# Issuing one low half of x behind a step's first addition, and one pair's first weight words behind an addition too

## The chip, the cores and the metric

The kernel runs on one core of a Trainium2 chip. The metric is the device time in microseconds (us) of one execution; shown runs of one kernel are compared by their median.

## The reference, cut to what matters

A channel attention over 6016 tokens and 256 channels, then two feed-forward layers with 2048 hidden units each:

```
s = kn.T @ qn / tau ; a = softmax(s) ; x = v @ a          # 6016 x 256
x = g1(x @ w_in) @ w_out      ; g1(h) = h * sigmoid(1.702 h)
x = g2(x @ w2_in) @ w2_out    ; g2(h) = max(0.01 h, h)
```

All inputs and the output are float32. The kernel splits each operand of a product into a rounded high half and a low half (the rest) and adds three products: high with high, low with high, high with low.

## The kernel before, in words

**Tiling.** The tokens are cut into six pairs of two column blocks, 512 columns wide each, 448 in the last pair. The two layers make twelve passes, numbered `i` from 0 to 11 (`i` of 6 and more is layer two). This text calls a pass a pair: pair 5 is the last of layer one, pair 11 the last of layer two. Each pair runs eight steps, `f` from 0 to 7; a step makes 2 x 128 hidden rows out of 256 channels. The hidden rows are made with seven block products in place of eight (a Strassen scheme): the blocks of x are combined beforehand (B11, T1, T2, T3 in `xa`, B21, B22, T4 in `xb`). From pair 3 on the output side works in the same way (`strassen_step`, L1292); pairs 1 and 2 use a simpler form (`step`, L1176).

**Engines.** TensorE (PE) makes all products. ScalarE (ACT) copies out of PSUM, applies the activation and makes high halves. VectorE (DVE) adds, subtracts and makes low halves (`subtract`, all recorded on L106, or L103 inside `halves`). Each engine works through its own instructions in the order in which the program issues them; that order is written out by hand (`manual_schedule`).

**One step of layer two** (L1292 to L1386), as it is issued: product A11, copy, product S2, copy to `tv`, product A12, its activation, product S3, copy to `tt`, `run_casts`, then `between(i, f)` (work for the next pair), product S1, and then the step's first addition on DVE, `add(g[:, 2], tt, pa)` at L1321. Behind it come the activation, the high half `g0[0]`, `next_stage()` (here the third stage of the step before: one DVE subtraction of 128x1024), `beyond(i, f)`, which empties the list `after`, then two output products, product S4, and the second addition `add(g[:, 1], tv, pa)`. S4 writes the same PSUM bank `pa` that the first addition reads.

**Next pair's x in layer two** (L1575 to L1601, called for pairs 5 to 10). The four blocks of the next pair lie in the staging tile `stg`. In steps 1 to 6 `more(j, n)` adds a block from HBM into block j of `stg` by an accumulating DMA on GpSimd's queue (POOL, L1579). `cast` makes a high half on ACT (L1512). `low` makes a low half on DVE, and `low_by_dma` makes it with an ACT copy (L1521) and an accumulating DMA on POOL's queue (L1524). In step 4 the order is: `low` of T3 out of block 1, `more(1, 0)` into the same block 1, `cast` of T1 out of block 0, `low_by_dma` of T1. In step 5, `cast(x, i, T2, 1)` reads block 1 after that `more`.

**Weights of layer two** are prepared during pairs 1 and 2. `begin_next` (L467) calls `words_of` for one weight piece: two DVE instructions put the words together (`bits`, L248 and L255), the load of a later piece is issued on SP, and `casts` gets the ACT work for `run_casts`. It is called at the end of each step of pair 1 and of steps 0 to 6 of pair 2. Between pair 1 and pair 2 `switch` (L1006) makes three blocks of `xb`: three casts on ACT and three low halves on DVE (L103).

**On the output side** `rest.pop(0)()` in `between` may transpose one output block on DVE (L1487) and store it with four DMAs (L1490); for pairs 7 to 10 one of these falls into step 4, ahead of `low`.

Of the kernel before, what the change touches and what calls it, by code (L numbers as in the profile page):

```python
# [17 lines left out]
def tile_kernel(  # L18
# [33 lines left out]
    NF = F // P // 2  # L52
# [39 lines left out]
    def bank(tag):  # L92
        return ps.tile([P, BLK], F32, tag=tag, name=tag)
# [28 lines left out]
    B11, T2, T1, T3 = range(4)  # L122
# [3 lines left out]
    with tc.manual_schedule():  # L126
# [324 lines left out]
        def run_casts():  # L451
            todo = list(casts)
            casts.clear()
            for item in todo:
                item()
# [11 lines left out]
        def begin_next():  # L467
            if words_left:
                words_of(words_left.pop(0))
# [636 lines left out]
                used.add(g)  # L1106

        coming = [prefetch(1, 1)]
        turn, streams = [], []

        def fetch():
            next(coming[0], None)
# [31 lines left out]
        def kept(tag, w):  # L1144
            return early.tile([P, BLK], F32, tag=tag, name=tag)[:, :w]
# [20 lines left out]
        def next_stage():  # L1166
            if stages:
                stages.pop(0)()
# [7 lines left out]
        def step(i, f):  # L1176

            layer, p = steps[i]
            w = width[p]
            product = products(i, f)  # L1180
            pa, pb = (bank(f"h{i}")[:, :w] for i in range(2))
            tp, tv, tt = (kept(tag, w) for tag in ("tp", "tv", "tt"))
            product(pa, A11, B11)
            nc.scalar.copy(pb, pa)
            while turn:
                turn.pop(0)()
            next_stage()
            slots.extend(lambda item=item, kc=kc: put(item, kc) for item in pend for kc in range(KC))
            pend.clear()
            outputs(2)  # L1190
            product(pb, S2, T2, more=True)
            nc.scalar.copy(tv, pb)
            product(pa, A12, B21, more=True)
            act(layer, tp, pa)
            hook("copy")
            next_stage()
            outputs(1)
            product(pb, S3, T3, more=True)
            nc.scalar.copy(tt, pb)
            run_casts()  # L1200
            between(i, f)
            product(pa, S1, T1)
            hook("burst")
            add(tt, tt, pa)
            if beside:
                beside.pop(0)()
            g11 = late.tile([P, 2, BLK], F32R, tag="gs", name="g11", bufs=2)[:, :, :w]
            g22 = late.tile([P, 2, BLK], F32R, tag="gq", name="g22")[:, :, :w]
            nc.scalar.copy(g11[:, 0], tp)
            subtract(g11[:, 1], tp, g11[:, 0].bitcast(F32))  # L1210
            act(layer, tt, tt)
            nc.scalar.copy(g22[:, 0], tt)
            next_stage()
            hook("one")
            beyond(i, f)
            outputs(2)
            hook("two")
            cc = late.tile([P, 2, BLK], F32, tag="cc", name="cc")[:, :, :w]
            product(pa, S4, B22, more=True)
            add(cc[:, 0], tv, pa)  # L1220
            close()
            hook("join")
            product(pb, A22, T4, more=True)
            act(layer, cc[:, 1], pb)
            subtract(g22[:, 1], tt, g22[:, 0].bitcast(F32))
            act(layer, cc[:, 0], cc[:, 0])
            if layer == 1:
                run_due()
                fetch()
                while streams:  # L1230
                    streams.pop()()
            outputs(len(slots))
            pend.append((layer, p, 1, f + NF, g22[:, 0], g22[:, 1]))
            pend.append((layer, p, 0, f, g11[:, 0], g11[:, 1]))

            def finish_step():
                gd = late.tile([P, 2, 2, BLK], F32R, tag="gd", name="gd", bufs=2)[:, :, :, :w]
                halves(gd[:, 0], gd[:, 1], cc)
                pend.append((layer, p, 1, f, gd[:, 0, 0], gd[:, 1, 0]))
                pend.append((layer, p, 0, f + NF, gd[:, 0, 1], gd[:, 1, 1]))  # L1240

            stages.append(finish_step)
            if f < NF - 1 or i == 1:
                begin_next()
            fetch()

        sets = [0]
# [266 lines left out]
        def low(to, i, n, j):  # L1514
            w = width[i % NPAIR]
            subtract(to[:, 1, n, :w], staged_x[i][:, j], to[:, 0, n, :w].bitcast(F32))
# [12 lines left out]
        def between(i, f):  # L1529
            if i < FIRST:  # L1530
                return
            k = NF * i + f
            if k >= NF * FIRST + 1:
                stream_in(k + 2)
            if k >= NF * FIRST + 2:
                stream_out(k + 1)
            if f == 0:
                if i == FIRST and i + 1 < NPAIR:
                    for n in range(2):
                        load_v(i + 1, n)  # L1540
                if i > FIRST:
                    cast(xbt, i, B22, 3)
                    cast(xbt, i, T4, t4_of(i))
                return
            if rest:
                rest.pop(0)()
            if f == 3 and i in (FIRST, NPAIR):
                raw_weights(steps[i][0])
            if i == LAST:
                return  # L1550
            i += 1
            x = xa[i % 2]
            first = 3
            if i < NPAIR:
                if f == 1 and i > FIRST + 1:
                    for n in range(2):
                        load_v(i, n)
                if f == 2:
                    move_in(i)
                    place_v(i, 0)  # L1560

                    def second_of_v():
                        place_v(i, 1)
                        for n in range(2, 4):
                            load_v(i, n)

                    after.append(second_of_v)
                if f == 3:
                    after.append(lambda: place_v(i, 2))
                if f == 4:  # L1570
                    place_v(i, 3)
            elif f == 1 and i not in staged_x:
                move_in(i)
            t = staged_x.get(i)
            if i >= NPAIR:  # L1575
                p = i - NPAIR

                def more(j, n):
                    nc.gpsimd.dma_start(out=t[:, j], in_=x2[p][:, n], accum_op=ALU.add)  # L1579

                if f == 1:
                    more(1, 3)
                if f == 2:
                    cast(x, i, B11, 0)
                    low_by_dma(x, i, B11, 0, x2[p][:, 0])
                if f == 3:
                    more(0, 1)
                    cast(x, i, T3, 1)
                if f == 4:
                    low(x, i, T3, 1)  # L1590
                    more(1, 0)
                    cast(x, i, T1, 0)
                    low_by_dma(x, i, T1, 0)
                if f == 5:
                    cast(x, i, T2, 1)
                if f == 6:
                    low(x, i, T2, 1)
                    more(1, 2)
                if f == 7:
                    cast(xbt, i, B21, 2)  # L1600
                return  # L1601
            if f == first:
                cast(x, i, B11, 0)
                low_by_dma(x, i, B11, 0)
            if f == first + 1:

                def sums_of_x():
                    subtract(t[:, 0], t[:, 1], t[:, 0])
                    cast(x, i, T1, 0)

                after.append(sums_of_x)
            if f == first + 2:
                low_by_dma(x, i, T1, 0)

                def sums_of_x():
                    subtract(t[:, 1], t[:, 3], t[:, 1])
                    cast(x, i, T3, 1)

                after.append(sums_of_x)
            if f == first + 3:  # L1620
                low_by_dma(x, i, T3, 1)

                def sums_of_x():
                    subtract(t[:, 0], t[:, 3], t[:, 0])
                    cast(x, i, T2, 0)

                after.append(sums_of_x)
            if f == first + 4:
                low(x, i, T2, 0)

                def sums_of_x():
                    subtract(t[:, 0], t[:, 2], t[:, 0])

                after.append(sums_of_x)
            if f == 7:
                cast(xbt, i, B21, 2)
                low_by_dma(xbt, i, B21, 2)

        def t4_of(i):
            return 1 if i >= NPAIR else 0  # L1640

        after = []
# [131 lines left out]
```

## Time and profile before

| what | value |
|---|---|
| median of 3 runs | 994.75 us (994.25 to 995.32) |
| the profiled execution | 994.62 us, of which the span of instructions is 992.8 us |
| PE busy | 987.3 us, 99% of the span, granted clock 1.0 |
| DVE, ACT, POOL busy | 889.0, 801.9 and 42.1 us |
| chain that ended last | PE 91%, DVE 4%, ACT 3%, issue 1%, DMA 1% |
| DMA | 221.80 MB, mean 223 GB/s |

The chain of waits is followed back from the last instruction: each piece is the work that set the time there. A matmul that starts late shows as a longer piece of PE. In the timeline a row's duration is that of the merged instructions of one kind, and the bracket gives the idle time of the engine before it and what ended it. A DMA's row on its queue is the time of its issue; the view of DMA issues gives the time from issue to landing.

### The profile page before, as it was taken

What the parts mean: (1) busy time and instruction counts of PE and PEld (TensorE: products, weight loads), DVE (VectorE), ACT (ScalarE), POOL (GpSimd) and SP (SyncE); (2) the same over time, 40 slices, a digit from 0 to 9 for tenths busy, and PEclk for the clock granted to TensorE, in tenths of its full rate; (3) what the DMA queues carried; (4) which work ended last, traced back from release to release, by engine and by line L of the source; (5) the groups of instructions that cost most, each with busy time, mean ns of one, the idle gap of its engine ahead of it and who ended that gap; (6) DMA issues with size and microseconds to landing.
All of it is one profiled execution on the core that took longest, in us unless ns stands there. A gap on an engine that the chain in (4) does not pass through costs nothing.

```text
span 992.8 us, 13244 instructions
## 1 busy us (share of the span) xinstructions
PE 987.3 (99%) x4454; PEld 825.8 (83%) x4454; DVE 889.0 (90%) x1264; ACT 801.9 (81%) x1298; POOL 42.1 (4%) x54
## 2 busy tenths in 40 slices
PE   9999999999999999999999999999999999999998
PEld 8888878888888878888998888888888888888997
DVE  7878898878878999999999999999999999999996
ACT  7687777788788897897897987887987997898782
POOL 0000000000000000000110010010010100100000
PEclk9999999999999999999999999999999999999999
DMA  9857679446865884975986975985986885885662
GB/s 346 279 149 248 236 265 305 160 149 201 247 199 159 275 248 159 277 219 158 324 252 221 291 227 175 259 249 182 260 242 195 240 240 182 247 254 180 199 196 40
DMA packets 160789, 221.80 MB, mean 223 GB/s; under 512 B 100817, under 2 KB 123345, under 8 KB 159697
## 3 DMA queue, kind: packets, MB, share of 16 engines
q1 hardware_dynamic: 149664, 207.98, 64.8%
q0 software_dynamic: 6768, 12.00, 7.6%
q10 hardware_dynamic: 4288, 0.98, 0.4%
q8 instruction: 35, 0.57, 0.2%
q14 instruction: 34, 0.27, 0.1%
HBM read 173.90 MB, written 42.73 MB: 218 GB/s over the span
## 4 chain that ended last, share of the span: by engine, by line
PE 91%; DVE 4%; ACT 3%; issue 1%; DMA 1%; SPq 0%; ACTq 0%
PE h L99 52%; PE y L99 19%; PE y L887 10%; PE y L1416 5%; PE y L611 4%; DVE gd L106 1%; DVE blocks L106 1%; DMA cv<-in_moe_w_in_dram 1%; ACT h L856 1%; ACT gd L1096 0%; ACT blocks L763 0%; DVE ta L255 0%; ACT wi L291 0%; DVE wt L106 0%; DVE wo L106 0%
## 5 line engine op out<-in xcount | busy, mean ns | idle before, releaser
L99 PE MATMUL h<-xa,wi 128*128 128x512 f32 (+1 forms) x861 | 226.9, 385 | 0.0
L99 PE MATMUL y<-g,wo 128*128 128x512 f32 (+1 forms) x840 | 209.8, 385 | 0.0
L99 PEld LDWEIGHTS h<-xa,wi 128*128 128x128 f32 x861 | 160.3, 188 | 32.2 <-DVE g L106 2.0
L99 PEld LDWEIGHTS y<-g,wo 128*128 128x128 f32 x840 | 156.8, 188 | 30.3 <-DVE g L106 0.4
L99 PE MATMUL h<-xb,wi 128*128 128x512 f32 (+1 forms) x645 | 168.4, 385 | 0.0
L106 DVE TENSOR_TENSOR g<-t,g 128x1024 fp32r<-128x1024 f32 (+1 forms) x140 | 166.8, 1192 | 0.0
L99 PEld LDWEIGHTS h<-xb,wi 128*128 128x128 f32 x645 | 120.6, 188 | 23.6 <-DVE g L106 1.7
L99 PE MATMUL h<-g,wo 128*128 128x512 f32 (+1 forms) x420 | 116.0, 384 | 0.0
L887 PE MATMUL y<-gd,wo 128*128 128x512 f32 (+1 forms) x402 | 100.5, 389 | 0.1
L858 ACT ACTIVATE g<-g 128x512 f32<-128x512 f32 (+1 forms) x92 | 57.7, 627 | 40.9 <-DVE g L106 40.1
L99 PEld LDWEIGHTS h<-g,wo 128*128 128x128 f32 x420 | 78.8, 188 | 14.3
L887 PEld LDWEIGHTS y<-gd,wo 128*128 128x128 f32 x402 | 75.0, 188 | 16.0 <-DVE gd L106 1.0
L106 DVE TENSOR_TENSOR g<-g,g 128x1024 fp32r<-128x1024 f32 (+1 forms) x70 | 83.6, 1194 | 1.0 <-ACT g L1324 0.4
L106 DVE TENSOR_TENSOR t<-g 128x1024 f32<-128x1024 f32 (+1 forms) x70 | 83.2, 1189 | 0.0
L99 PE MATMUL h<-xa,wa 128*128 128x512 f32 x288 | 78.8, 391 | 0.0
L1353 ACT CAST g<-t 128x1024 fp32r<-128x1024 f32 (+1 forms) x70 | 72.2, 1032 | 3.4 <-DVE t L106 2.6
L1324 ACT CAST g<-g 128x1024 fp32r<-128x1024 f32 (+1 forms) x70 | 72.2, 1031 | 2.2
L1372 ACT CAST g<-t 128x1024 fp32r<-128x1024 f32 (+1 forms) x70 | 71.7, 1025 | 0.0
L99 PE MATMUL h<-xb,wa 128*128 128x512 f32 x240 | 64.9, 391 | 0.1
L106 DVE TENSOR_TENSOR g<-tt,h 128x512 f32<-128x512 f32 (+1 forms) x70 | 46.9, 670 | 19.6 <-ACT tt L1316 17.6
L99 PEld LDWEIGHTS h<-xa,wa 128*128 128x128 f32 x288 | 53.4, 188 | 12.1 <-ACT blocks L763 1.0
L106 DVE TENSOR_TENSOR t<-raw,t 128x512 f32<-128x512 f32 (+1 forms) x70 | 47.5, 679 | 7.6 <-ACT g L1353 0.5
(206 smaller groups left out, 1523.1 us busy)
## 6 DMA issues: line engine op xcount, KB each, us to landing
wi<-w2a SPq DMA_DIRECT2D x48, 896.0 KB, 6.2
wo<-w2o SPq DMA_DIRECT2D x46, 768.0 KB, 4.6
wi<-w1a SPq DMA_DIRECT2D x24, 896.0 KB, 5.8
wo<-w1o SPq DMA_DIRECT2D x24, 768.0 KB, 4.8
cv<-in_moe_w_in_dram SPq DMA_DIRECT2D x32, 256.0 KB, 3.6
cv<-in_moe_w_out_dram SPq DMA_DIRECT2D x32, 256.0 KB, 3.5
w1a<-wa SPq DMA_DIRECT2D x8, 896.0 KB, 3.6
stg<-x SPq DMA_DIRECT2D x5, 1024.0 KB, 4.7
```

The costliest lines, as they stand in the source:

```text
L99: nc.tensor.matmul(dst, lhsT=w, rhs=x, start=start, stop=stop, skip_group_check=more)
L106: nc.vector.tensor_tensor(out=out, in0=in0, in1=in1, op=op)
L611: nc.tensor.matmul(s_ps[h][:, :C], lhsT=t[:, 1, r, h * P:(h + 1) * P], rhs=t[:, 0, r, :], start=(j == 0 and r == 0), stop=(j == last and r ...
L856: nc.scalar.activation(out=out, in_=in_, func=AF.Gelu_apprx_sigmoid)
L858: nc.scalar.activation(out=out, in_=in_, func=AF.Prelu, alpha=0.01)
L887: nc.tensor.matmul(ys[key][kc], lhsT=ws[x], rhs=y, start=first and n == 0, stop=closing or (final and n == 2), skip_group_check=closing,)
L1324: nc.scalar.copy(g0[0], g[:, 0::2])
L1353: nc.scalar.copy(g1[0], t13)
L1372: nc.scalar.copy(g2[0], mine["t24"])
L1416: nc.tensor.matmul(sums[i, M1], lhsT=x, rhs=y, start=False, stop=True, skip_group_check=True,)
```

## The change

In layer two's step 4, `low` of T3 and `more(1, 0)` are put into the list `after`, which `beyond` empties behind the first addition and the third stage; the `cast` and `low_by_dma` of T1 stay where they were, so that on POOL's queue the DMA of T1 now stands ahead of `more(1, 0)`. In `step`, the `begin_next` at the end of pair 1's last step is put into a list `behind`, which step 0 of pair 2 empties after the high half of `tt`, followed by a `run_casts()`.

```diff
-        turn, streams = [], []
+        turn, streams, behind = [], [], []
...
             act(layer, tt, tt)
             nc.scalar.copy(g22[:, 0], tt)
+            if behind:
+                behind.pop(0)()
+                run_casts()
             next_stage()
...
             stages.append(finish_step)
-            if f < NF - 1 or i == 1:
+            if f < NF - 1:
                 begin_next()
+            elif i == 1:
+                behind.append(begin_next)
             fetch()
...
                 if f == 4:
-                    low(x, i, T3, 1)
-                    more(1, 0)
+
+                    def behind_addition():
+                        low(x, i, T3, 1)
+                        more(1, 0)
+
+                    after.append(behind_addition)
                     cast(x, i, T1, 0)
                     low_by_dma(x, i, T1, 0)
```

## Rows read from the trace of the kernel before

**Rows 1.** The page, busy us (share of the span) and instructions of each engine

```profile
PE 987.3 (99%) x4454; PEld 825.8 (83%) x4454; DVE 889.0 (90%) x1264; ACT 801.9 (81%) x1298; POOL 42.1 (4%) x54
```

**Rows 2.** The chain of waits: start us, us, what; step 4's last hidden products, three pairs

```profile
573.54 2.72 PE h L99 x12
...
649.78 2.96 PE h L99 x12
...
879.30 2.90 PE h L99 x12
```

**Rows 3.** Timeline, pair 7, step 4: start us, us, engine, line, operation, tiles

```profile
648.42 0.65 DVE L106 TENSOR_TENSOR xa<-stg,xa 128x512 fp32r<-128x512 f32 x1
...
648.99 0.63 ACT L1521 ACTIVATE xa<-xa 128x512 fp32r<-128x512 f32 x1
648.99 0.68 DVE L106 TENSOR_TENSOR g<-tt,h 128x512 f32<-128x512 f32 x1
649.58 0.86 POOL L1579 DMA_DIRECT2D stg<-x  x1 [15.58 <-ACT xa L1512]
...
649.73 1.23 PEld L99 LDWEIGHTS h<-xb,wi 128*128 128x128 f32 x6 [0.37 <-DVE g L106]
...
650.12 1.22 POOL L1524 DMA_DIRECT2D xa<-stg  x1
...
650.73 0.69 DVE L106 TENSOR_TENSOR g<-tv,h 128x512 f32<-128x512 f32 x1
...
651.90 0.84 PE L99 MATMUL h<-xa,wi 128*128 128x512 f32 x3
```

**Rows 4.** Timeline, pair 7, step 5, and the first output products of step 6

```profile
657.41 0.63 ACT L1512 CAST xa<-stg 128x512 fp32r<-128x512 f32 x1
657.61 0.69 DVE L106 TENSOR_TENSOR g<-tt,h 128x512 f32<-128x512 f32 x1 [0.53 <-ACT tt L1316]
...
658.33 0.64 ACT L858 ACTIVATE g<-g 128x512 f32<-128x512 f32 x1 [0.29 <-DVE g L106]
...
659.00 1.05 ACT L1324 CAST g<-g 128x1024 fp32r<-128x1024 f32 x1
...
660.18 1.22 DVE L106 TENSOR_TENSOR g<-g,g 128x1024 fp32r<-128x1024 f32 x1
...
661.42 1.52 PE L99 MATMUL y<-g,wo 128*128 128x512 f32 x6
```

**Rows 5.** Timeline, from pair 1 to pair 2

```profile
227.61 0.42 DVE L248 TENSOR_SCALAR ta<-cv 128x512 int32<-128x512 int32 x1
...
228.67 1.89 DVE L103 TENSOR_TENSOR xb<-stg,xb 128x512 fp32r<-128x512 f32 x3
228.77 1.15 PE L99 MATMUL h<-xb,wa 128*128 128x512 f32 x3
...
229.41 0.19 PEld L99 LDWEIGHTS h<-xb,wa 128*128 128x128 f32 x1 [0.46 <-DVE xb L103]
```

**Rows 6.** DMA issues of POOL, KB, us to landing: pair 7, then pairs 5, 10, 8

```profile
stg<-x POOLq DMA_DIRECT2D x1, 256.0 KB, 4.3
xa<-stg POOLq DMA_DIRECT2D x1, 256.0 KB, 9.5
...
xa<-stg POOLq DMA_DIRECT2D x1, 256.0 KB, 8.0
...
xa<-stg POOLq DMA_DIRECT2D x1, 224.0 KB, 7.9
...
xa<-stg POOLq DMA_DIRECT2D x1, 256.0 KB, 7.3
```

**Rows 7.** DMA issues of POOL, pair 7, step 6: one transfer with none beside it

```profile
stg<-x POOLq DMA_DIRECT2D x1, 256.0 KB, 3.7
```

**Rows 8.** Timeline, pair 5: the DMA of T1's low half, and the cast of T2

```profile
501.50 0.88 POOL L1524 DMA_DIRECT2D xa<-stg  x1
...
507.86 0.63 ACT L1512 CAST xa<-stg 128x512 fp32r<-128x512 f32 x1
```

## The prediction

> **What bounds the kernel now.** I read the page's busy times first: PE is busy 987.3 of 992.8 us, DVE 889.0 and ACT 801.9 [rows 1]. So only time in which PE stands can be won, and DVE and ACT have little room to catch up in. Then the chain of waits, which is PE in 91% of the span: the reader compares the same piece from pair to pair. The twelve last hidden matmuls of a step take 2.72 us where nothing disturbs them (pair 6), but 2.96 in step 4 of pair 7, as also of pairs 8 and 9, and 2.90 in pair 10 [rows 2]. Then the timeline at such a place: PE's weight load stands idle 0.37 us and is released by DVE [rows 3]. DVE's first addition, which frees the bank that S4 wants, starts at 648.99 because the low half of T3 ran ahead of it from 648.42. In step 5, where no low half stands there, DVE is itself idle 0.53 us until ACT's `tt` is there [rows 4]. The same view from pair 1 to pair 2 shows three matmuls in 1.15 us that take 0.84 elsewhere, the third held by a low half of `xb` on DVE, which had the weight words ahead of it from 227.61 [rows 3, 5].
>
> **The change, part by part.**
>
> *The low half, moved behind the addition.* The addition can start when `tt` is ready, 0.57 us earlier in the queue than the 648.99 it has now, less the little that `tt` still asks. The excess of the chain's pieces goes: 3 x (2.96 - 2.72) + (2.90 - 2.72) = 0.90 us [rows 2]. Pairs 5 and 6 have no transposition ahead and no such excess (pair 6's piece is the undisturbed 2.72), so nothing is won there. What is late next on DVE is the second addition: the same three instructions (addition, third stage, low half) stand ahead of it in another order, so it starts where it does now, at 650.73, or 0.1 later, and ends by 651.5. The next step's first matmul, which overwrites that bank, is at 651.90 and would come 0.24 earlier, at 651.66 [rows 3]. I take 0 for it; the price if the cover is gone is some 0.05 us at each of six places.
>
> *The weight words, moved behind pair 2's first addition.* Two DVE instructions from 227.61 leave the stretch ahead of the three low halves that start at 228.67 [rows 5]; these may start up to 1.06 us earlier, and 0.46 is wanted. Gain 1.15 - 0.84 = 0.31 us. The same DVE, ACT and SP work now comes later in the same step, where ACT has its casts to make either way; it is the same sum of work, so I take nothing, with 0.3 us (the whole gain) as the upper end of a loss.
>
> *The transfer behind the low half.* This is the expensive part. `more(1, 0)` must wait for the low half, since it writes the block that this reads. Now the low half starts at 648.42 and ends at 649.07, and POOL issues the transfer 0.51 later, at 649.58 [rows 3]. Behind the change the first addition starts near 648.53; what now follows it after the third stage does so 650.73 - 648.99 = 1.74 later, so the low half starts at 650.27. It ends at 650.92, and the transfer is issued at 651.42, 1.84 us later than now. And it loses its place: T1's DMA, which needs ACT's copy of 648.99 alone, is issued first. Its receiver is the ACT cast of T2 in step 5, at 657.41 now [rows 4] and 657.17 with the 0.24 won.
>
> How long the second of two such transfers takes is in the trace, with the roles reversed: the one issued first at 649.58 landed in 4.3 us, at 653.9, the one issued 0.54 us behind it took 9.5, to 659.6 [rows 3, 6]. Alone such a transfer takes 3.7 [rows 7]. So from both sides: 651.42 + 3.7 = 655.1, which costs nothing, or 659.6, when both are through now. I take the second, as the same two transfers beside the same traffic are the nearest row.
>
> The Trainium skill bears on this choice: "DMA: Bandwidth & Descriptors", section "Queues, rings and completion order", states that on each DMA engine descriptors are consumed in ring order and that an engine takes turns between queues packet by packet. By that rule the moved transfer stands behind T1's on every ring and the sum is the one below; without it the gain alone would be left. The trace agrees as far as it goes: 9.5 us for the second against 4.3 for the first [rows 6].
>
> What ACT's lateness costs PE: behind the cast of T2 ACT has 0.29 us of idle time (before 658.33). Its high half then ends at 659.00 + 1.05 = 660.05, and DVE takes it at 660.18, which leaves some 0.05 beside the usual hand-over. DVE's low half ends at 661.40, and the third matmul of 661.42 + 1.52 x 2/6 = 661.9 wants it: 0.41 more after the hand-over [rows 4]. Slack 0.29 + 0.05 + 0.41 = 0.75 us; what is later than that PE pays.
>
> The cast comes 657.41 - 650.12 = 7.29 us after T1's present issue in pair 7, and within 0.03 of that in pairs 6, 8, 9 and 10; in pair 5 507.86 - 501.50 = 6.36 [rows 3, 4, 8]. With T1's present landing as the moved transfer's:
> pair 7: 9.5 - 7.29 + 0.24 = 2.45 late, 1.70 paid;
> pair 5: 8.0 - 6.36 = 1.64 late, 0.89 paid (the same slack taken for its narrower step);
> pair 10: 7.9 - 7.29 + 0.18 = 0.79 late, 0.04 paid;
> pair 8: 7.3 - 7.29 + 0.24 = 0.25, nothing; pairs 6 and 9 landed sooner still [rows 6].
> Cost 2.63 us.
>
> **The sum.** Against the profiled execution's 994.62 us (span 992.8 and 1.8 around it): - 0.90 - 0.31 + 2.63 = + 1.42, so 996.04. The median of the runs is 994.75, 0.13 higher: 996.2 us.
>
> **The rivals.**
>
> *A, the forecast*: the moved transfer lands about when T1's did, 995.3 to 996.9.
>
> *B, the transfer is hidden anyway.* It lands 1.84 us later than it did, 653.9 + 1.8 = 655.7, well ahead of 657.17, if it flows beside T1's or if T1's, now starting on a free queue, is through in the 3.7 us of a transfer alone. For it: in no pair is the first of two held up much (4.3 against 3.7). Against it: the second was, each time, 7.3 to 9.5 in the shown rows. Only the gain stays: 994.62 - 1.21 = 993.4, on the median's basis 993.5 us.
>
> *C, slower: both transfers are through later than now.* Place: ACT's cast of T2 in step 5. T1's DMA goes out when ACT's copy is done, 648.99 + 0.63 and the issue, near 649.9, so the queue starts its first transfer 0.3 us later than the present 649.58 [rows 3]; the second is issued 1.5 behind in place of 0.54, so engines that were through with the first stand without work of it for a while. Each 0.1 us of this costs 0.1 in pairs 5, 7 and 10, and past 0.5 in pair 8 too [rows 6]. From 0.2 it decides: 3 x 0.2 more than A is past 996.7. With 0.7: 5 gives 1.59, 7 gives 2.40, 10 gives 0.74, 8 gives 0.20, together 4.93, less 1.21 is + 3.7: 998.5 us. Against it: the queue's end is set by other traffic at its own times as much as by its start.
>
> *D, it does not do what it says*: something else holds the first addition as long (`tt` alone does so in step 5), and the transfer is in time: no gain in layer two, 994.4 us.
>
> **How the numbers follow.** A 0.38, B 0.28, C 0.28, D 0.06. The range 993.0 to 998.6 holds A, B with half a us of scatter and most of C; A's own range is 995.3 to 996.9. Faster or slower by 0.2% is 2.0 us, about what a measurement of this kernel can tell from no change: under 992.8 or over 996.7. Faster: nothing in the sum reaches it, 0.04. Slower: C and the upper edge of A, 0.36. The rest, 0.60.
>
> **What would show it.** In the changed kernel step 4's piece of pairs 7 to 10 is 2.72 us and the three matmuls at pair 2's begin take 0.84: the gain. POOL's queue has T1's DMA ahead of `more(1, 0)`, the latter near 1.8 us later in its step. If A or C holds, ACT is idle ahead of the cast of T2 in step 5 of pairs 7 and 5, released by a DMA, and PE stands at the first output products of step 6. If that ACT wait is under 0.75 us everywhere, A falls and B holds; if it is over 0.75 in pair 8 as well, C. If step 4 still shows 2.96, the gain was mis-attributed.

## The result: slower, and the profile after

The changed kernel takes 1004.04 us (median of 4 runs, 1001.74 to 1005.50) against 994.52 us of the kernel before in the same comparison: ratio 1.0093 [1.0080, 1.0106]. The profiled execution took 1005.5 us, its span 1003.7, 10.9 more than before. The forecast was 996.2, the end of its range 998.6.

The page of the changed kernel, the chain that ended last, by engine:

```profile
PE 80%; DVE 7%; DMA 6%; ACT 4%; issue 2%; POOL 0%; SPq 0%; ACTq 0%; POOLq 0%; DVEq 0%
```

PE is busy 989.4 us and DVE 889.1, within 2.1 us of [rows 1], so the work is the same. What has changed is who sets the end: PE's share of the chain fell from 91% to 80%, and DMA's rose from 1% to 6%. The view of waits names the receiver: ACT's cast of T2 (L1517, L1512 before), six waits, one in each pair from 5 to 10; in the kernel before no such line stands among ACT's waits.

```profile
ACT xa L1517 <- DMA stg<-x: 13.9, 6, 5.7
...
PE y L99 <- ACT g L1329: 5.7, 3, 4.2
```

(Columns: us in total, times, longest.) The timeline shows both sides of the change, first at pair 2's begin, then in pair 5 and pair 7:

```profile
228.91 0.84 PE L99 MATMUL h<-xb,wa 128*128 128x512 f32 x3
...
501.05 0.87 POOL L1529 DMA_DIRECT2D xa<-stg  x1 [14.08 <-ACT xa L1526]
...
513.33 0.62 ACT L1517 CAST xa<-stg 128x512 fp32r<-128x512 f32 x1 [5.71 <-DMA stg<-x]
...
655.47 0.63 ACT L1526 ACTIVATE xa<-xa 128x512 fp32r<-128x512 f32 x1
...
656.39 0.86 POOL L1529 DMA_DIRECT2D xa<-stg  x1 [15.93 <-ACT xa L1526]
...
657.65 0.34 SPq L1027 DMA_DIRECT2D wi<-w2a  x1
657.72 0.86 POOL L1584 DMA_DIRECT2D stg<-x  x1 [0.46 <-DVE xa L106]
...
658.08 0.53 PEld L99 LDWEIGHTS h<-xa,wi 128*128 128x128 f32 x3 [0.21 <-DVE g L106]
...
666.69 0.62 ACT L1517 CAST xa<-stg 128x512 fp32r<-128x512 f32 x1 [2.85 <-DMA stg<-x]
...
668.97 0.73 PE L99 MATMUL y<-g,wo 128*128 128x512 f32 x2 [1.07 <-ACT g L1329]
```

The three matmuls at pair 2's begin take 0.84 us in place of 1.15 [rows 5], and the transfer now stands second on POOL's queue, as meant. But one row is here that the prediction did not look at: SP's load of weights, 896 KB, is issued 0.07 us ahead of the moved transfer. The view of DMA issues says what became of the two transfers of pair 5 and then of pair 7, and what POOL's queue (q0) moved in two stretches of pair 7, from 657.72 to 662.5 and from 662.5 to 667:

```profile
xa<-stg POOLq DMA_DIRECT2D x1, 256.0 KB, 9.3
stg<-x POOLq DMA_DIRECT2D x1, 256.0 KB, 11.1
...
xa<-stg POOLq DMA_DIRECT2D x1, 256.0 KB, 4.7
stg<-x POOLq DMA_DIRECT2D x1, 256.0 KB, 8.9
...
q1 hardware_dynamic: 1322, 0.74, 71.9%
q0 software_dynamic: 144, 0.26, 34.4%
...
q0 software_dynamic: 144, 0.26, 32.4%
```

In the first stretch q0 moved 0.26 MB, which is T1's DMA alone, while 0.74 MB of q1 went by; the moved transfer's 0.26 MB came only in the second. It had moved nothing 4.8 us after its issue. In [rows 6] the same transfer, first on its queue, had landed after 4.3. Pairs 5, 6 and 8 are like this one (nothing of it 4.4 to 4.8 us after the issue). In pairs 9 and 10 it was under way sooner (in pair 9 q0 had moved 0.41 MB in the 4.8 us, T1's 0.26 and part of it) and landed after 7.9 and 6.6 us all the same.

Pair 5 is a case of its own in part: T1's DMA itself landed later there than before (9.3 us for 8.0 [rows 6]), and of the two transfers' 0.52 MB all but 0.01 had moved by 510.3, while the last of it landed 3 us later. In e6_cast_later, an experiment below, the same transfer of pair 5 landed after 6.5 us. Why it took 11.1 here no run shows.

How much each pair paid is read from the chain: the same piece, step 6's first hidden products (step 7's in pair 5), in the kernel after, with the two longest pieces of DMA,

```profile
502.18 11.12 DMA stg<-x
...
526.83 3.04 PE h L99 x15
...
657.72 8.95 DMA stg<-x
...
671.45 3.43 PE h L99 x15
...
826.90 3.41 PE h L99 x15
...
903.28 1.81 PE h L99 x8
```

and in the kernel before (654.10 is step 5 of pair 7):

```profile
520.72 3.04 PE h L99 x15
...
654.10 3.40 PE h L99 x15
...
662.94 3.40 PE h L99 x15
...
815.94 3.40 PE h L99 x15
...
892.39 3.40 PE h L99 x15
```

The differences are 6.11 us (pair 5), 8.51 (7), 10.96 (9) and 10.89 (10). Into pair 5 the changed kernel came 0.45 ahead (501.05 against 501.50 [rows 8]), into pair 7 it came 6.48 late (ACT's copy at 655.47 against 648.99 [rows 3]). So, net of the gain in step 4:

| pair | 5 | 6 | 7 | 8 and 9 | 10 |
|---|---|---|---|---|---|
| paid, us | 6.56 | 0.37 | 2.03 | 2.45 | -0.07 |
| forecast, us | 0.89 | 0 | 1.46 | -0.48 | -0.14 |

The forecast's row is its own terms, cost less gain. The pairs sum to 11.34, less the 0.45 from ahead of them 10.89: the whole difference of the spans.

Pair 5 holds a second loss. The windows of PE there, and then one each of two experiments below, e2_low_only and e8_break_changed (columns: stretch, us, busy time and instructions of PE, its weight loads, DVE, ACT and POOL, then the granted clock, DMA's share and GB/s):

```profile
512.00:515.40 3.40, 0.00 (x0) 0.00 (x0) 0.00 (x0) 2.04 (x4) 0.00 (x0) 1.00 0.54 217
515.40:517.00 1.60, 1.14 (x3) 0.72 (x4) 1.57 (x2) 1.57 (x4) 0.00 (x0) 0.67 0.05 22
517.00:519.00 2.00, 2.00 (x7) 1.74 (x7) 1.86 (x4) 1.27 (x2) 0.00 (x0) 0.50 0.00 0
...
516.00:518.00 2.00, 2.00 (x7) 1.80 (x6) 1.90 (x4) 0.90 (x2) 0.00 (x0) 0.50 0.00 0
...
665.00:667.00 2.00, 1.15 (x4) 0.67 (x5) 1.70 (x2) 1.97 (x5) 0.00 (x0) 1.00 0.53 222
```

After PE had stood 4.21 us, the granted clock went from 1.00 to 0.50, the 1.2 GHz level, and PE issued 7 matmuls in those 2 us; the next 2 us, at 0.91, have 11. The length of the wait alone does not tell when this happens: in e2_low_only the clock was at 0.50 behind a wait of PE of 1.49 us (the fourth row), in e8_break_changed it stayed at 1.00 behind one of 1.75 (the last row), as it did here behind pair 7's 1.07.

### The profile page after: what moved, and what is told of

Read it like the earlier page. It is cut to its first block, busy times and chain, and to the rows that moved or that the text cites. A ratio compares the mean times of both kernels' runs of the same rounds, so it can differ in the third digit from the quotient of the medians.

```text
span 1003.7 us, 13243 instructions
## 1 busy us (share of the span) xinstructions
PE 989.4 (99%) x4454; PEld 825.0 (82%) x4454; DVE 889.1 (89%) x1264; ACT 801.3 (80%) x1298; POOL 41.9 (4%) x54
## 4 chain that ended last, share of the span: by engine, by line
PE 80%; DVE 7%; DMA 6%; ACT 4%; issue 2%; POOL 0%; SPq 0%; ACTq 0%; POOLq 0%; DVEq 0%
PE h L99 45%; PE y L99 16%; PE y L887 10%; PE y L1421 5%; DMA stg<-x 5%; PE y L611 3%; DVE g L106 2%; DMA qk<-in_k_dram 1%; DVE gd L106 1%; DVE t L106 1%; DVE blocks L106 1%; ACT h L856 1%; DMA cv<-in_moe_w_in_dram 1%; ACT gd L1096 0%; ACT blocks L763 0%
## 5 line engine op out<-in xcount | busy, mean ns | idle before, releaser
L99 PE MATMUL y<-g,wo 128*128 128x512 f32 (+1 forms) x840 | 212.6, 388 | 7.7 <-ACT g L1329 5.7
L106 DVE TENSOR_TENSOR g<-g,g 128x1024 fp32r<-128x1024 f32 (+1 forms) x70 | 83.5, 1194 | 11.6 <-ACT g L1329 11.3
```

Source lines behind the costliest of these rows:

```text
L99: nc.tensor.matmul(dst, lhsT=w, rhs=x, start=start, stop=stop, skip_group_check=more)
L106: nc.vector.tensor_tensor(out=out, in0=in0, in1=in1, op=op)
```

## The experiments

Theories at the start: the moved transfer lands late and ACT waits for it, because it is second on its queue (the forecast's rivals A and C); because POOL's transfers are held up while DVE runs without a break; or because of something else that is issued there. Ratios are to the kernel before, with 95% intervals. "Alone" below means that T1's DMA is out of the way, as in the experiment e4_alone.

**The two parts by themselves.** One kernel has only the words' part, with step 4 as before; the other only step 4's part.

```diff
 e1_words_only
-                    after.append(behind_addition)
+                    low(x, i, T3, 1)
+                    more(1, 0)
 e2_low_only
-            if f < NF - 1:
+            if f < NF - 1 or i == 1:
                 begin_next()
-            elif i == 1:
-                behind.append(begin_next)
```

> Only the weight words of the third pair are moved; layer two stays as before. Both theories of the loss (see the next runs) say that this half is not it. The prediction's term: the three matmuls at pair 2's begin go from 1.15 to 0.84 us, so about 0.3 us less than before, 994.2 us; not more than 0.1% away from before. If this half cost anything, over 995.5.

> Only the low half of T3 and the DMA behind it are moved; the words stay. Both theories: the whole loss is here, 1003 to 1005 us, with ACT idle 3 to 6 us ahead of the cast of T2 in step 5 of pairs 5, 7, 8 and 9. If the loss came from the two moves together, under 998.

Measured: words only 993.97 us, 0.9993 [0.9984, 1.0002]; step 4 only 1003.75, 1.0088 [1.0071, 1.0105]. All of the loss is in step 4's part; the words' 0.31 us is too small for the measured times to tell but stands in the timeline. The chain of e2_low_only has the moved transfer in it in every pair from 5 to 10; in pair 5 its piece is 8.42 us, so pair 5's 11.12 above is not the same in every execution.

**Is ACT's wait the path?** The moved transfer is left as it is, and only its reader, the cast of T2, is put behind step 5's first addition.

```diff
-                    cast(x, i, T2, 1)
+                    after.append(lambda: cast(x, i, T2, 1))
```

> The changed kernel, but step 5's ACT cast of T2, which waits for the moved transfer, is issued behind the step's first addition, its activation and its high half. If ACT's wait at the head of the step is the way by which the late transfer reaches PE, the step's own ACT work is no longer behind it: the cast comes some 2 us later in the queue, most of the wait goes, 994 to 998 us. If the loss has another way (GpSimd's transfers slowing the weight loads, say), near 1004 us.

Measured: 994.19, 1.0000 [0.9988, 1.0012]. The loss is gone, though the transfer lands no sooner: 10.4 us after its issue in pair 7. So the late transfer costs through this one instruction: a cast that stands in ACT's order ahead of step 5's activation.

**Place on the queue.** In e3_order_back T1's DMA goes behind the moved transfer; in e4_alone it goes to step 6.

```diff
 e3_order_back
                         more(1, 0)
+                        low_by_dma(x, i, T1, 0)
 e4_alone
                     cast(x, i, T1, 0)
-                    low_by_dma(x, i, T1, 0)
...
                     more(1, 2)
+                    low_by_dma(x, i, T1, 0)
```

> The changed kernel, but the low half of T1 (its ACT copy and its DMA) is also issued behind the first addition, behind the moved transfer, so that the moved transfer is first on its queue again. Place-in-queue theory (the prediction's): it then lands some 4.3 us after its issue, ahead of the cast of T2, and only the gain is left: 993.5 us. Held-start theory (a transfer of this queue that is issued when DVE begins its long run of subtractions out of SBUF does not begin to move data until that run has a break, some 4 to 5 us after the issue, whatever stands ahead of it): the transfer still lands 6 to 9 us after its issue and the time stays near 1000 to 1004 us.

> The changed kernel, but the low half of T1 (ACT copy and DMA) is made in step 6 instead of step 4, so the moved transfer has no other transfer of its queue near it. Place-in-queue theory: alone such a transfer lands in 3.7 us, the cast of T2 never waits, 993.5 us. Held-start theory: its first data still moves 4 to 5 us after the issue, it lands 6 to 8 us after it, ACT waits 0 to 2 us in step 5 of most pairs, 996 to 1003 us.

Measured: e3_order_back 996.25, 1.0020 [1.0009, 1.0031], ACT still waits 5.4 us in four pairs; e4_alone 994.96, 1.0007 [0.9998, 1.0016], waits 2.8 us in four. The place costs most of the loss. But alone on its queue the transfer still needs 4.8 to 7.1 us over the six pairs, where [rows 7] had 3.7. Pair 7 of e4_alone, the timeline, and then the DMA view of the 3 us behind the issue (651.91 to 654.91; the first line is the busy share in 40 slices, in tenths):

```profile
651.62 0.47 SPq L1027 DMA_DIRECT2D wi<-w2a  x1
...
651.91 0.86 POOL L1584 DMA_DIRECT2D stg<-x  x1 [17.47 <-ACT g L1329]
```

```profile
DMA  9999998743999099874960040950456962792699
...
q1 hardware_dynamic: 1029, 0.56, 97.1%
...
stg<-x POOLq DMA_DIRECT2D x1, 256.0 KB, 6.3
```

There is no line of q0 at all: nothing of the transfer had moved after 3 us, though it stood alone, and though the 16 engines were under a tenth busy in some of the slices. Something holds its start, and the place on the queue is not it.

**A theory that fell: DVE without a break.** The Trainium skill, "SBUF — State Buffer", section "SBUF: two separate sides", warns that while DVE runs an instruction in a two-port mode GpSimd can't write a DMA's descriptors, so that the DMA looks blocked by DVE. The same page counts `tensor_tensor`, which DVE's subtractions are, among the instructions without such a mode (section "Who interferes with whom"), so it does not foretell a hold here. The theory went further than the page: DVE runs here one instruction behind the other, and any such run might do it. I put work in step 5 that makes a break in DVE's subtractions (two fills), or none (two more subtractions of the same size), on the changed kernel and on e4_alone; then a copy out of PSUM that has DVE wait for ACT.

```diff
 e5_memset_changed, e5_memset_alone (e5_subtract_*: two subtract(...) in their place)
+                if f == 4 and NPAIR - 1 <= i < LAST:      # step 4's stage, issued in step 5
+                    nc.vector.memset(ones, 1.0)
+                    nc.vector.memset(ident, 0.0)
                 subtract(t13, g[:, 1:3], g[:, 0:2])
 e8_break_changed, e8_break_alone
             nc.scalar.copy(pb, pa)
+            if f == 5 and NPAIR - 1 <= i < LAST:
+                nc.vector.tensor_copy(ones[:, :64], pa[:, :64])
```

> The changed kernel with two fills (memset) of 128x128 put on DVE in step 5 of pairs 5 to 10, ahead of the first subtraction of its first stage, some 1.3 us after the moved transfer is issued. A fill reads no SBUF. Held-start theory: the break lets the transfer start about 1.6 to 2 us after its issue instead of 4 to 5; it is still second on its queue and lands about 5 to 7 us after its issue instead of 6.6 to 11; the time falls from 1004 to 996 to 999 us. If the late start has nothing to do with DVE, the fills only add DVE time: 1004 us or more.

> The control to the run before: in place of the two fills two subtractions of 128x128 whose both inputs lie in SBUF, at the same place. Held-start theory: no break, the transfer starts as late as in the changed kernel or a little later, 1003 to 1006 us. If any short DVE instruction at that place were enough, the same time as with the fills.

> The kernel in which T1's low half is made in step 6 (the moved transfer alone on its queue), with the two fills of 128x128 in step 5. Held-start theory: first data of the moved transfer 1.5 to 2.1 us after its issue in all six pairs, landing 3.7 to 5 us after it, no ACT wait ahead of the cast of T2; 993.5 to 995 us. Otherwise first data still 3.5 to 4.3 us after the issue in four of six pairs.

> The control to the run before: two subtractions of 128x128 out of SBUF in place of the fills. Held-start theory: first data 3.5 us or more after the issue in most pairs, landing 6 to 7.5 us after it, ACT waits of up to 1.5 us ahead of the cast of T2; 994.5 to 996 us.

> The kernel with T1's low half in step 6 (the moved transfer alone on its queue), with one DVE copy of 128x64 out of PSUM in step 5 of pairs 5 to 10, ahead of the first stage. The fills did not shorten the start. If a break must be one in which DVE reads PSUM or stands idle, as it is in the places where such a transfer starts after 1.6 us, the first data now moves 1.6 to 2.2 us after the issue in all pairs and it lands 3.7 to 5 us after it. If DVE has no part in it, 3.5 to 4.9 us to the first data in most pairs, as with the fills.

> The same DVE copy out of PSUM in the changed kernel. With the break theory the moved transfer starts earlier but stays second on its queue: it lands 5 to 7 us after its issue, 996 to 1000 us. If DVE has no part, 1001 us or more.

Measured on the changed kernel: fills 1000.86, 1.0068 [1.0051, 1.0085]; subtractions 1000.91, 1.0059 [1.0040, 1.0078]; PSUM copy 1003.57, 1.0090 [1.0076, 1.0104]. Alone: fills 994.29, 1.0008 [0.9996, 1.0021]; subtractions 995.54, 1.0008 [0.9997, 1.0018]; PSUM copy 998.46, 1.0037 [1.0022, 1.0052]. Fills and subtractions can't be told apart. Why both are some 3 us better than the changed kernel without them I did not follow up. The last pair settles the theory: in pair 7 of e8_break_alone DVE does nothing for 0.65 us while the transfer is due, from 1.2 to 1.9 us after its issue (issued at 653.87, 0.29 behind the load; DVE's copy starts at 655.74), and it lands after 6.2 us, no sooner than in e4_alone. (That kernel is slower because PE now waits six times for ACT's `tv`, 1.9 us together.) So these runs show no hold by DVE's subtractions, which agrees with the page's own condition; its warning itself is not tried by any run here.

**The weight load.** What all these kernels share is the row of SP next to the transfer. I left out one of the loads for pairs 5 to 10, so that a step computes with the weights of the step before it: in the one kernel the load for step 6, in the other that for step 7.

```diff
         def stream_in(k):
             i, f = divmod(k, NF)
+            if f == 6 and NPAIR - 1 <= i < LAST:      # e9_other_load_changed: f == 7
+                iw[i, f] = iw[i, f - 1]
+                return
```

> The changed kernel with the weight load that SP issues in step 4 (step 6's hidden-layer weights) left out for pairs 5 to 10; step 6 then uses step 5's weights, so this part of the result is another. Behind-the-load theory: the moved transfer is held because the 16 DMA engines first serve the 896 KB load that was issued 0.3 us ahead of it. Without the load its first data moves about 1.6 us after its issue, it lands 4 to 5.5 us after it though it is still second on its queue, ACT does not wait, 993 to 994.5 us. If it is held by its place behind T1's DMA or by anything else of that step, it lands 6.5 us or later and the time stays over 1000 us.

> The control to the run before: the load left out is that of step 7's hidden-layer weights, which SP issues in step 5 of the same pairs, some 9 us later (step 7 then uses step 6's weights). Behind-the-load theory: nothing changes for the moved transfer, 1002 to 1006 us. If it is only the amount of traffic, most of the loss goes here too, under 998 us.

Measured: without step 6's load 1005.31, 1.0105 [1.0074, 1.0137]; without step 7's 993.31, 0.9985 [0.9974, 0.9995]. The two came out the other way round than I had named them: I had taken the load beside the transfer to be step 6's. The timeline shows that it is step 7's. SP runs ahead of the program's steps, and a load waits only until its buffer is free. Step 6's load stands some 9 us ahead of that (648.81 and 657.65 in the changed kernel); leaving out its 896 KB takes none of the loss away, so it is not the amount of traffic in the step. In e9_no_load_changed a load still stands beside the transfer (SP at 652.48, POOL at 652.55), and ACT waits six times. In e9_other_load_changed there is none between 649.24 and 656.75; pair 7's timeline, and the landings of T1's DMA and the moved transfer:

```profile
649.24 2.19 SPq L1498 DMA_DIRECT2D out_dram<-o  x4
650.63 0.87 POOL L1532 DMA_DIRECT2D xa<-stg  x1 [15.92 <-ACT xa L1529]
651.96 0.86 POOL L1587 DMA_DIRECT2D stg<-x  x1 [0.47 <-DVE xa L106]
...
656.75 0.34 SPq L1045 DMA_DIRECT2D wo<-w2o  x1
```

```profile
xa<-stg POOLq DMA_DIRECT2D x1, 256.0 KB, 4.2
stg<-x POOLq DMA_DIRECT2D x1, 256.0 KB, 4.9
```

Second on its queue as in the changed kernel, the transfer lands after 4.9 us (4.2 to 5.1 over the six pairs), and ACT never waits for it. This takes away the load's bytes as well as its place, which the next two runs keep.

**The same load, issued behind the transfer.** The low half and `more(1, 0)` stand directly behind the first addition's high half, ahead of the third stage (1.2 us of DVE), so the transfer goes out before the load. Once with T1's DMA away, once with it in front.

```diff
             nc.scalar.copy(g0[0], g[:, 0::2])
+            while at_once:
+                at_once.pop()()
             next_stage()
...
-                    after.append(behind_addition)
+                    at_once.append(behind_addition)
                     cast(x, i, T1, 0)
-                    low_by_dma(x, i, T1, 0)           # e10_low_ahead_alone only; to step 6
```

> The kernel with T1's low half in step 6, and in step 4 the low half of T3 and its DMA directly behind the first addition, ahead of the third stage, 1.1 us earlier than in the change: the transfer is then issued about 0.8 us ahead of the weight load instead of 0.3 behind it. Behind-the-load theory: its first data moves 1.6 us after the issue in all pairs, it lands 3.7 to 5 us after it and ACT never waits; 993.3 to 994 us. If the start is held by something else of the step, 3.5 us or more to the first data in most pairs.

> The same, with T1's DMA in step 4 as in the change, ahead of the moved transfer on its queue. POOL's issue of T1's takes 0.86 us from about 1.3 us ahead of the load, so the moved transfer is issued about 0.4 us ahead of the load, but as the second. Place alone (the prediction's term): it lands 6 to 9.5 us after T1's issue, 995 to 997 us. If the second of two in quick succession is held behind the load as well, it lands 9 us or more after its issue and the time is 1000 us or more.

Measured: alone 993.73, 0.9991 [0.9982, 1.0000], no wait of ACT on it; with T1's DMA in front 1000.28, 1.0063 [1.0046, 1.0080], 8.9 us of waits in five pairs. Pair 7 of e10_low_ahead_alone, timeline, the DMA view of the 3 us behind the issue (649.96 to 652.96), and the chain in step 4:

```profile
649.96 0.86 POOL L1586 DMA_DIRECT2D stg<-x  x1 [16.34 <-ACT g L858]
...
650.80 0.35 SPq L1027 DMA_DIRECT2D wi<-w2a  x1
```

```profile
q0 software_dynamic: 87, 0.18, 52.4%
...
stg<-x POOLq DMA_DIRECT2D x1, 256.0 KB, 4.7
```

```profile
649.41 2.79 PE h L99 x12
...
653.59 3.40 PE h L99 x15
```

Against e4_alone the low half and its DMA stand ahead of the third stage, which puts the transfer 0.84 us ahead of the load, not 0.29 behind it. In the first 3 us 0.18 of its 0.26 MB move, not none, and it lands 1.6 us sooner. With T1's DMA in front this is lost again. There, in pair 7, the moved transfer is issued at 652.59, 0.54 us behind T1's; its issue takes 1.22 us in place of 0.86 and ends at 653.81, behind the whole of the load's issue (653.31 to 653.65), and it lands 9.1 us after its issue.

The kept traces tell more than these two runs: what goes with the held start is not which issue begins first but which ends first. In pair 7 of e3_order_back the load's issue begins 0.29 us ahead of the transfer's, as in e4_alone, but takes 2.08 us and ends last. Its timeline, and the DMA view of the 3 us behind the transfer's issue (652.41 to 655.41):

```profile
652.12 2.08 SPq L1027 DMA_DIRECT2D wi<-w2a  x1
652.41 0.86 POOL L1584 DMA_DIRECT2D stg<-x  x1 [17.47 <-ACT g L1329]
```

```profile
q0 software_dynamic: 112, 0.22, 44.9%
```

The transfer moved 0.22 MB in these 3 us and landed after 4.4. The start times of POOL's packets say the same in all the traces. Where a `more` was issued within 1 us of such a load in pairs 5 to 10 and was first on its queue, its first data moved 3.53 to 4.86 us after the begin of its issue in the 43 cases in which the load's issue ended first, and 1.56 to 1.66 us after it in the 10 in which its own did. Both kinds stand in e4_alone: in pair 9 SP was still busy with stores, the load came 0.49 us behind the transfer, and this landed after 4.8 us; in the other five pairs it took 5.8 to 7.1. In the changed kernel the load's issue ended first in pairs 5 to 8, and last in pairs 9 and 10, where it took 1.20 and 0.93 us; there the transfer started right behind T1's DMA, and still landed too late beside the load.

**A version without the loss.** Step 4 as before; only the transposition of pairs 7 to 10, which pushes the low half into the addition, goes behind it, with the words' part kept.

```diff
-                rest.pop(0)()
+                if f == 4 and i >= NPAIR:
+                    after.append(rest.pop(0))
+                else:
+                    rest.pop(0)()
```

> The same gain sought without moving the transfer: the weight words behind pair 2's first addition as in the change, and in step 4 of layer two the transposition of the output block (and its store) goes behind the first addition, while the low half of T3 and its DMA stay ahead of it. The first addition loses the same length of DVE work ahead of it, and the accumulating transfers keep their times: step 4's piece 2.72 us in pairs 7 to 10, 0.9 + 0.3 us less than before, 993.3 us. If a store that starts 2 us later disturbs another transfer, 994.5 or more.

Measured: 993.85, 0.9990 [0.9981, 0.9999]. It beats both kernels, by about what the stalls were worth; 0.1% is at the edge of what can be told, and against the words alone (993.97) the transposition's own part can't be told from the times. In the chain pair 7's piece of step 4 is 2.78 us, for 2.96 before and 2.72 expected.

## Why the prediction was wrong, step by step

- *The words*: right. 0.31 forecast, 1.15 to 0.84 in the timeline.
- *The low half behind the addition*: right in kind, half in size. Pairs 7 to 9 were to gain 0.24 each. In e10_low_ahead_alone step 4's last hidden products and what follows them take 653.59 - 649.41 = 4.18 us against 654.10 - 649.78 = 4.32 before [rows 2], a gain of 0.14; the changed kernel's own pair 10 gives 0.13 (894.44 - 890.32 = 4.12 against 883.55 - 879.30 = 4.25). Pair 6, which had no excess to win, lost 0.12. The rest goes back at the place that I costed at nothing, with 0.05 a place as the price if the cover is gone: the second addition is now late for the next step's first matmul (in the changed kernel PE's weight load stands 0.21 us, released by DVE, at 658.08).
- *The order on POOL's queue and the time of issue*: right. Pair 7's issue in its own time is 657.72 - 6.48 = 651.24, forecast 651.42.
- *How lateness reaches PE*: right. Pair 7's cast is 666.69 - 6.48 - 657.41 = 2.80 late, and PE paid 2.03: a slack of 0.77, forecast 0.75.
- *The landing* is the step that failed: "With T1's present landing as the moved transfer's". The moved transfer's landing was copied, pair by pair, from another transfer, T1's DMA, whose issue in pair 7 had ended ahead of the weight load's (650.12 + 1.22 = 651.34, the load's begin 651.41). In pair 7 the size was nearly met (657.72 + 8.95 - 6.48 = 660.19, forecast 659.6), but by luck: T1's DMA was through after 4.7 us, and then nothing of POOL's queue moved until 662.5. In pair 5 it was not: 502.18 + 11.12 + 0.45 = 513.75, forecast 509.5. In pairs 8 and 9 the sum had no cost at all, and 2.45 were paid. The term was 2.63 us in all; measured it is 11.3 net of the gain. What stands in its place: the issue was moved onto the weight load, and a transfer whose issue ends behind the issue of this load starts late, in pairs 5 to 8 more than 4 us after its issue. It could have been read: the forecast has the issue at 651.42, and the timeline before has a load at 651.41. That a POOL transfer just behind a load lands late is there too, at 541.37, as these rows of the kernel before show:

```profile
541.05 0.55 SPq L1027 DMA_DIRECT2D wi<-w2a  x1
541.37 0.86 POOL L1579 DMA_DIRECT2D stg<-x  x1 [24.02 <-PE h L99]
...
651.41 0.34 SPq L1027 DMA_DIRECT2D wi<-w2a  x1
```

```profile
stg<-x POOLq DMA_DIRECT2D x1, 256.0 KB, 7.7
```

That one landed after 7.7 us where no other POOL transfer was near it, and nothing waited for it then.

- *Pair 5's clock*: in no term. The cast there is 513.33 - 507.86 + 0.45 = 5.92 late; less 0.75 of slack, 5.17 would be paid. 6.56 were. The other 1.39 us go with the stretch at the lower clock: in the chain the 15 hidden products behind it, from 518.43, take 3.53 us where the next step's take 3.04, and the four output products ahead of them 1.86 where six take 1.22.
- *The rivals*: C had the right place and sign (ACT's wait, and pair 8 as well), with another mechanism, a gap on POOL's own queue. T1's DMA did not land later, as C has it, but sooner in pairs 6 to 10 (in pair 7 4.7 us for 9.5 [rows 6]); later only in pair 5 (9.3 for 8.0). B, the hidden transfer, is what e9_other_load_changed shows, once the load is gone.

Shown: the loss is ACT's wait for this transfer (e6), it goes with the load beside it (e9), and the order of the two issues goes with when the transfer starts (e4 against e10, and the traces). The full loss has both, the load beside the transfer and T1's DMA in front of it. With the load alone 0.07% is left (e4), with T1's DMA alone nothing (e9). Getting the transfer's issue begun 0.72 us ahead of the load is not enough behind T1's DMA: 0.63% is left (e10_low_ahead_changed). The hold is also not all of it: in pairs 9 and 10 of the changed kernel the start was not held, and ACT still waited 1.78 and 0.51 us. Still open: why a transfer whose issue ends second starts only when most of the load is through, and pair 5's late last packets.

## What to carry to other kernels

When a step is moved, write down the new issue time of each of its DMAs and look at what every other queue issues there: here the forecast's own time was 0.01 us from a large load's, and which of the two issues ended first made the difference between a start after 1.6 us and one after 3.5 or more. The duration of another transfer, even on the same queue, holds only for its own place among the loads. And where a late transfer can't be avoided, move its reader: putting one cast behind the addition took back the whole 0.9%.

## What was not expected of the hardware

- A GpSimd transfer of 256 KB whose issue ended behind that of SP's load of 896 KB had moved nothing after 3 us (e4_alone, pair 7, alone on its queue) and 4.8 us (the changed kernel, pair 7, behind T1's DMA), while the other queue moved 0.56 and 0.74 MB. Where its issue ended ahead of the load's it moved 0.18 MB in its first 3 us (e10_low_ahead_alone), and 0.22 (e3_order_back) though the load's issue had begun first. In e4_alone's wait the 16 engines were under a tenth busy in some slices, so they weren't short of time.
- The Trainium skill, "DMA: Bandwidth & Descriptors", section "Queues, rings and completion order", says that an engine takes turns between the queues, a packet from each. By that the transfer would have begun among the load's packets. In e4_alone it did not, which suggests that its descriptors were not there yet; no view here shows descriptors.
- Behind a wait of PE of 4.21 us the granted clock was at 0.50 for a stretch, and so it was behind one of 1.49 (e2_low_only) and one of 1.18 us (e9_no_load_changed); behind one of 1.75 us (e8_break_changed) it stayed at 1.00.
- SP's loads run ahead of the program's steps by their buffers, so which load stands beside a transfer is read from the timeline, not from the code.
